# Attention followed by a SoLU layer: the transposed tiles come back from DRAM by one transfer into all 128 partitions

## The chip, the cores and the metric

The kernel runs on one core of a Trainium2 chip. The metric is the device time of one execution in microseconds (us), smaller is better. A profiled execution has its own time, and its span, from the first to the last instruction in the trace, lies a little below that.

## The reference, cut to what matters

```python
# chunked attention: 4 batches, 8 heads, 768 positions, 64 features per head
for c in range(nc):                      # chunks of 32 queries
    k_full = concat(mem_k, k[l_start:r_end])      # at most 8 + 16 + 32 + 8 = 64 keys
    scores = scale * q_c @ k_full.T
    a = exp(scores - max(scores)); a = a / (sum(a) + 1e-09)
    out[c] = a @ v_full
x = out as (3072 tokens, 512)
# SoLU layer with layer norm, d_ff = 1024
h = x @ w_in
solu = h * softmax(h)
ln = (solu - mean) / sqrt(var + 1e-06) * g_ln
return ln @ w_out                        # (3072, 512)
```

## The kernel before

The 3072 tokens are 24 tiles of 128. Attention is done by items: item 0 is tile 0, item 1 is tile 1, and each of the items 2 to 12 is two tiles. The two products of the SoLU layer are done tile by tile.

**Products in two parts.** The operands of `hidden` (x times w_in) and `project` (ln times w_out) are split into a rounded high part and a low part, both in the format fp32r, and each product is three matmuls: high by high, high by low, low by high. A tile has 8 such triples in `hidden` (four blocks of 128 features of x, two halves of 512 hidden columns) and 8 in `project`. In `hidden` the activations are the stationary operand and 512 columns of w_in the moving operand, which is read contiguously.

**Transposing.** Three kinds of data must have their features on the partitions before TensorE (PE) can use them: the probabilities p, the attention output x and the SoLU output u. Two ways exist.

- On PE, by a product with the identity (steps `PT`, `XT`, `UT`). The order uses it for the items 0 to 3 (p and x) and for u of the tiles 0 to 3.
- Through DRAM, for all else (9 items of p, 9 of x, 20 tiles of u, so 38 times). `square` lets VectorE (DVE) transpose every 32 x 32 block of the 128 x 1024 tile; `write` sends it to DRAM in one transfer of 512 KB; `read` brings it back in four transfers of 128 KB, the d-th into the partitions 32d to 32d+31. After that, partition 32d+n holds feature n of block d.

**Order.** The program text is a hand-written list of steps, `ORDER`, and every engine executes its own instructions in that order. Names in it: `Lq Lk Lv` loads of q, k, v; `S` scores, `M` row maximum, `Bm` subtracts it, `X` exponential, `Z` row sums; `Pt Pw Pr` (and `Xt Xw Xr`, `Ut Uw Ur`) square, write and read; `V` probabilities times values, `N` divides by the row sums; `XH XL UH UL` high and low parts; `G` one triple of `hidden`; `Hm He Hu` softmax of the hidden row; `C Sq Dn` centre, square and scale; `O` one triple of `project`; `Os St` scaling and store. The list names the engine of some steps by a letter: @V VectorE, @S ScalarE, @G GpSimd. The list is the same before and after.

**Queues.** Writes, reads and loads are all issued by SyncE (SP), one after the other in the order of the list. The stores of the output are issued by ScalarE. An issue waits on semaphores for its source and its buffer, and what is behind it on the same engine waits with it.

Lines that the change touches: 315 to 321 (`read`), 373 to 379 (`below_max`), 385 to 392 (`row_sum`), 424 to 431 (`norm`), 469 to 486 (`hidden`), and the host's layout of v, w_in and w_out.

Of the kernel before, what the change touches and what calls it, by code (L numbers as in the profile page):

```python
# [15 lines left out]
ALU = mybir.AluOpType  # L16
AX = mybir.AxisListType

P = 128
CHUNK, LEFT, RIGHT = 32, 16, 8  # L20
NEG = -1.0e30
SQ = 32
SLOTS, HALVES, RAWS, ROUNDED = 7, 6, 4, 8
SINGLES = 2
SPLIT = {0: 2}


# [2 lines left out]
ORDER = """  # L30
# [59 lines left out]
def chunked_attention_then_solu_kernel(  # L90
# [22 lines left out]
    nc = tc.nc  # L113
    D = P // 2
    NP_ = w_in.shape[0] // (2 * D)
    NT = out.shape[0] // P
    NCH = P // CHUNK
    LINE = kw.shape[0] // (NT * P * NP_)
    KEYS = P // 2
    DM, DF = w_in.shape  # L120
    items = [(t, 1) for t in range(SINGLES)] + [(t, 2) for t in range(SINGLES, NT, 2)]
    NC_ = DM // P
    NF = DF // P
    HALF = DF // 2
    TPB = 6
# [14 lines left out]
    away = {}  # L140
# [12 lines left out]
    def get(*key):  # L153
        return held[key][0]

    def used(*key):
        held[key][1] -= 1
        if held[key][1] == 0:
            buf, _, kind = held.pop(key)
            if kind == "raw":  # L160
                rest[0] -= 1
                if rest[0] < RAWS:
                    free["slot"].extend([buf[:, 0:W], buf[:, W:2 * W]])
                    return
            free[kind].append(buf)
# [13 lines left out]
    w_in_h = const.tile([P, NC_, DF], F32R, name="w_in_h")  # L179
    w_in_l = const.tile([P, NC_, DF], F32R, name="w_in_l")  # L180
# [66 lines left out]
    def cut(ap, i, x):  # L247
        n = ap.shape[1] // SPLIT.get(i, 1)
        return ap[:, x * n:(x + 1) * n]
# [4 lines left out]
    def w_load(i):  # L254
        raw = take("raw", ("raw", i), 2 * SPLIT.get(i, 1)).bitcast(U32)
        nc.sync.dma_start(raw, w_in32[i] if i < NC_ else w_out32[i - NC_])
# [39 lines left out]
    def home(i):  # L296
        return "slot" if items[i][1] == 2 else "half"
# [17 lines left out]
    def read(name):  # L315
        def step(i):
            t = get(name + "t", i).rearrange("p (q e) -> p q e", q=4)
            a = away[name, i].rearrange("(q n) (d e) -> q n d e", q=4, d=4)
            for d in range(4):
                nc.sync.dma_start(t[SQ * d:SQ * d + SQ], a[:, :, d].rearrange("q n e -> n q e"))  # L320
        return step

    def by_block(ap):
# [32 lines left out]
    def by_head(i):  # L356
        n = items[i][1]
        return get("s", i)[:, :, 0:n * HALF // 2].rearrange("p r (n k) -> p r n k", k=KEYS)

    def row_max(i):  # L360
# [9 lines left out]
        nc.vector.tensor_reduce(nmax, s, axis=AX.X, op=ALU.max, negate=True)  # L370
        used("s", i)

    def below_max(i):
        n = items[i][1]
        nmax = get("nmax", i)[:, 0:2 * n * NP_].rearrange("p (r n) -> p r n", r=2).unsqueeze(3)
        a = take(home(i), ("p", i), 2).rearrange("p (n r k) -> p r n k", r=2, k=KEYS)
        nc.vector.tensor_tensor(a, by_head(i), nmax.broadcast_to([P, 2, n * NP_, KEYS]), ALU.add)
        used("s", i)
        used("nmax", i)

# [3 lines left out]

    def row_sum(i):
        s = take("per_head", ("rinv", i), 1)[:, 0:2 * items[i][1] * NP_]
        nc.vector.tensor_reduce(  # L387
            s, get("p", i).rearrange("p (n k) -> p n k", k=KEYS), axis=AX.X, op=ALU.add
        )
        nc.vector.tensor_scalar(s, s, 1e-9, None, ALU.add)  # L390
        nc.vector.reciprocal(s, s)
        used("p", i)
# [31 lines left out]
    def norm(i):  # L424
        n = items[i][1]
        rinv = get("rinv", i)[:, 0:2 * n * NP_].rearrange("p (n r) -> p r n", r=2).unsqueeze(3)
        x = take(home(i), ("x", i), 1).rearrange("p (n r d) -> p r n d", r=2, d=D)
        xp = get("xp", i)[:, :, 0:n * HALF // 2].rearrange("p r (n k) -> p r n k", k=D)
        nc.vector.tensor_tensor(x, xp, rinv.broadcast_to([P, 2, n * NP_, D]), ALU.mult)
        used("xp", i)  # L430
        used("rinv", i)

# [36 lines left out]
    def hidden(t, c, half):  # L469
        if c == 0 and half == 0:  # L470
            take("two", ("h", t), 2)
        u, odd = divmod(t, 2)
        h = get("h", t)
        x = [
            get(n, u).rearrange("p (t c n) -> p t c n", t=2, n=P)[:, odd, c]
            for n in ("xh", "xl")
        ]
        w = (w_in_h, w_in_l)
        for i, (a, b) in enumerate(((0, 0), (0, 1), (1, 0))):
            nc.tensor.matmul(  # L480
                h[:, half], x[a], w[b][:, c, half * HALF:(half + 1) * HALF],
                start=c == 0 and i == 0, stop=c == NC_ - 1 and i == 2,
            )
        if c == NC_ - 1 and half == 1:
            used("xh", u)
            used("xl", u)
# [65 lines left out]
    def store(t):  # L552
# [24 lines left out]
def _layout(q, k, v, mem_k, mem_v):  # L577
    import numpy as np

    B, H, S, D = q.shape  # L580
    M = mem_k.shape[2]
    NPAIR = H // 2
    NCH = S // CHUNK
    KEYS = M + LEFT + CHUNK + RIGHT
    TPB = S // P
    CPT = P // CHUNK
    NT = B * TPB

    qT = q.reshape(B, NPAIR, 2, TPB, P, D).transpose(0, 3, 2, 5, 1, 4)
    qT = qT.reshape(NT, 2 * D, NPAIR, P)  # L590

    def padded(x):
        z = np.zeros((B, H, LEFT, D), x.dtype)
        return np.concatenate([z, x, z[:, :, :RIGHT]], 2)

    kp, vp = padded(k), padded(v)

    lines = []
    for t in range(TPB):
        x = kp[:, :, t * P:t * P + P + LEFT + RIGHT]  # L600
        mid = P - CHUNK
        lines.append(np.concatenate([x[:, :, :CHUNK], mem_k, x[:, :, CHUNK:mid], mem_k, x[:, :, mid:]], 2))
    kw = np.stack(lines, 1).reshape(B, TPB, NPAIR, 2, -1, D).transpose(0, 1, 3, 5, 2, 4)
    kw = kw.reshape(NT, 2 * D, NPAIR, -1)

    wins = []
    for c in range(NCH):
        x = vp[:, :, c * CHUNK:c * CHUNK + KEYS - M]
        e = 0 if c % 2 else CHUNK
        wins.append(np.concatenate([x[:, :, :e], mem_v, x[:, :, e:]], 2))  # L610
    vw = np.stack(wins, 2).reshape(B, NPAIR, 2, TPB, CPT, KEYS, D).transpose(0, 3, 2, 5, 1, 4, 6)
    vw = vw.reshape(NT, 2 * KEYS, NPAIR, CPT, D)
    def by_item(x):
        n = x.shape[0]
        late = x[SINGLES:].reshape((n - SINGLES) // 2, 2, P, -1).transpose(0, 2, 1, 3)
        return np.concatenate([x[:SINGLES].ravel(), late.ravel()])

    return by_item(qT), by_item(kw), by_item(vw)
# [28 lines left out]
```

## Time and profile before

| what | value |
|---|---|
| median of 3 runs | 359.84 us (356.36 to 359.94) |
| profiled execution, its own time | 359.48 us |
| span of its trace | 357.7 us |
| PE busy in it | 325.8 us |
| DVE busy in it | 219.7 us |

PE is TensorE's matmuls, PEld its loads of the stationary operand, DVE is VectorE, ACT ScalarE, POOL GpSimd, SP SyncE; SPq is SyncE issuing transfers. L312 is line 312 of the kernel. Names of buffers stand without their numbers, as out<-in. [...]

### The profile page before, as it was taken

The page shows a single profiled execution, that of the slowest core. Times are in us where ns is not written, and L with a number is a line of the kernel's source. Part 1 is how long each engine was busy: PE and PEld are TensorE (multiplying, and loading weights), DVE is VectorE, ACT ScalarE, POOL GpSimd, SP SyncE. Part 2 cuts the span into 40 slices and gives each one's busy share as a digit, 9 for nine tenths or more (in the row PEclk, how much of TensorE's full clock was granted, in tenths as well). Part 3 has the DMA queues.
Part 4 walks back from the last instruction along what each step waited for, and adds up shares of the span by engine and source line. Part 5 has one row for each costly group of instructions (what it writes and reads, how often), then busy time and mean ns, then how long its engine had stood idle before and what let it go on. Part 6 is the DMA issues. An engine that isn't in the chain of part 4 may idle for free.

```text
span 357.7 us, 9973 instructions
## 1 busy us (share of the span) xinstructions
PE 325.8 (91%) x4324; PEld 263.7 (74%) x4324; DVE 219.7 (61%) x264; ACT 130.0 (36%) x189; POOL 138.9 (39%) x173
## 2 busy tenths in 40 slices
PE   1569999999997999979999899999959999999995
PEld 1557887888785877857887678888647888888884
DVE  1589999968966964756955386564466654037300
ACT  3256375542422414122322334422225064232521
POOL 0226061442318263752500834220523746625160
PEclk9969999999998999998999999999969999999999
DMA  7999925576897876689959679866651547435621
GB/s 296 420 422 400 405 78 199 198 252 192 302 306 218 245 267 214 220 233 353 268 191 263 194 216 382 286 188 188 212 210 60 184 114 226 128 129 173 226 90 59
DMA packets 37771, 82.31 MB, mean 230 GB/s; under 512 B 4320, under 2 KB 23776, under 8 KB 35296
## 3 DMA queue, kind: packets, MB, share of 16 engines
q1 hardware_dynamic: 34272, 75.39, 62.8%
q10 hardware_dynamic: 3456, 6.29, 4.7%
q8 instruction: 34, 0.56, 0.6%
q14 instruction: 9, 0.07, 0.1%
HBM read 55.45 MB, written 26.21 MB: 228 GB/s over the span
## 4 chain that ended last, share of the span: by engine, by line
PE 61%; DMA 18%; DVE 12%; SPq 3%; ACT 3%; issue 2%; POOL 1%; DVEq 0%; POOLq 0%; ACTq 0%
PE one L540 28%; PE two L480 23%; DMA out<-half 5%; PE two L347 4%; PE two L415 3%; SPq L320 3%; DMA q<-in_qT 2%; DMA raw<-p_away 2%; DMA k<-in_kw 2%; DVE per_head L387 2%; DMA p_away<-raw 2%; DMA raw<-x_away 1%; DMA slot<-x_away 1%; PE two L203 1%; PE two L333 1%
## 5 line engine op out<-in xcount | busy, mean ns | idle before, releaser
L480 PE MATMUL two<-w_in_h,fr 128*128 128x512 f32 x384 | 143.0, 405 | 6.8 <-DVE fr L219 4.6
L540 PE MATMUL one<-w_out_h,fr 128*128 128x512 f32 x384 | 138.1, 396 | 0.1
L480 PEld LDWEIGHTS two<-w_in_h,fr 128*128 128x128 f32 x384 | 73.4, 192 | 26.1 <-DVE fr L219 5.4
L540 PEld LDWEIGHTS one<-w_out_h,fr 128*128 128x128 f32 x384 | 72.7, 189 | 16.8 <-DVE fr L219 0.5
L480 PE MATMUL two<-w_in_l,fr 128*128 128x512 f32 x192 | 76.2, 397 | 0.2 <-DVE w_in_l L219 0.2
L540 PE MATMUL one<-w_out_l,fr 128*128 128x512 f32 x192 | 75.2, 391 | 0.0
L489 DVE TENSOR_REDUCE per_row<-two 128x1 f32<-128x1024 f32 x24 | 29.1, 1212 | 28.9 <-PE two L480 28.8
L548 ACT ACTIVATE half<-one,per_row 128x512 f32<-128x512 f32 x24 | 16.5, 687 | 82.2 <-PE one L540 80.8
L480 PEld LDWEIGHTS two<-w_in_l,fr 128*128 128x128 f32 x192 | 36.9, 192 | 7.7 <-DVE w_in_l L219 0.6
L540 PEld LDWEIGHTS one<-w_out_l,fr 128*128 128x128 f32 x192 | 36.5, 190 | 7.3
L219 POOL TENSOR_TENSOR fr<-raw,fr 128x1024 fp32r<-128x1024 f32 x13 | 31.2, 2403 | 17.4 <-ACT fr L214 16.6
L347 PE MATMUL two<-k,q 64*32 64x64 f32 x1536 | 19.6, 237 | 14.5 <-DMA k<-in_kw 7.6
L347 PEld LDWEIGHTS two<-k,q 64*32 64x32 f32 x1536 | 17.1, 111 | 18.8 <-issue 17.9
L216 POOL TENSOR_SCALAR fr<-raw 128x1024 fp32r<-128x1024 f32 x11 | 11.6, 1051 | 47.1 <-DVE slot L304 18.1
L219 POOL TENSOR_TENSOR fr<-slot,fr 128x1024 fp32r<-128x1024 f32 x9 | 21.5, 2391 | 18.1 <-DMA slot<-u_away 10.7
L494 ACT ACTIVATE slot<-two,per_row 128x1024 f32<-128x1024 f32 x12 | 13.4, 1118 | 30.6 <-DVE per_row L489 30.6
L494 ACT ACTIVATE raw<-two,per_row 128x1024 f32<-128x1024 f32 x12 | 13.4, 1115 | 27.7 <-DVE per_row L489 21.4
L216 POOL TENSOR_SCALAR fr<-slot 128x1024 fp32r<-128x1024 f32 x8 | 8.4, 1052 | 32.4 <-DMA slot<-u_away 15.3
L504 DVE CUSTOM_DVE_ANT_0 slot<-two,slot 128x1024 f32<-128x1024 f32 x12 | 14.7, 1222 | 8.1 <-ACT slot L494 8.1
L504 DVE CUSTOM_DVE_ANT_0 raw<-two,raw 128x1024 f32<-128x1024 f32 x12 | 14.5, 1206 | 7.7 <-ACT raw L494 6.2
L370 DVE TENSOR_REDUCE per_head<-two 128x16 f32<-128x1024 f32 (+1 forms) x13 | 14.8, 1135 | 5.0 <-PE two L347 4.7
L304 DVE STREAM_TRANSPOSE raw<-slot 128x1024 f32<-128x1024 f32 x10 | 12.4, 1238 | 8.1 <-POOL slot L516 5.9
(88 smaller groups left out, 372.9 us busy)
## 6 DMA issues: line engine op xcount, KB each, us to landing
v<-in_vw SPq DMA_DIRECT2D x11, 1024.0 KB, 8.5
k<-in_kw SPq DMA_DIRECT2D x11, 672.0 KB, 6.8
out<-half ACTq DMA_DIRECT2D x24, 256.0 KB, 3.0
u_away<-raw SPq DMA_DIRECT2D x12, 512.0 KB, 3.5
raw<-u_away SPq DMA_DIRECT2D x48, 128.0 KB, 3.4
q<-in_qT SPq DMA_DIRECT2D x11, 512.0 KB, 7.8
raw<-in_w_in SPq DMA_DIRECT2D x4, 1024.0 KB, 11.3
raw<-in_w_out SPq DMA_DIRECT2D x4, 1024.0 KB, 9.2
```

What stands on the lines that cost most here:

```text
L216: nc.gpsimd.tensor_scalar(out, in_, 1.0, 0.0, ALU.mult, ALU.add)
L219: (nc.gpsimd if on == "G" else nc.vector).tensor_tensor(out, a, b, ALU.subtract)
L304: nc.vector.transpose(t, src.rearrange("p (m d n) -> p d m n", d=4, n=SQ))
L320: nc.sync.dma_start(t[SQ * d:SQ * d + SQ], a[:, :, d].rearrange("q n e -> n q e"))
L347: nc.tensor.matmul(s[32 * j:32 * j + 32, r, t, g], q[rows, o + t, g, 32 * j:32 * j + 32], k[rows, o + t, g, START[j]:START[j] + KEYS], sta ...
L370: nc.vector.tensor_reduce(nmax, s, axis=AX.X, op=ALU.max, negate=True)
L480: nc.tensor.matmul(h[:, half], x[a], w[b][:, c, half * HALF:(half + 1) * HALF], start=c == 0 and i == 0, stop=c == NC_ - 1 and i == 2,)
L489: nc.vector.tensor_reduce(take("per_row", ("hm", t), 1), flat(get("h", t)), axis=AX.X, op=ALU.max, negate=True)
L494: nc.scalar.activation(take("slot", ("u", t), 2), flat(get("h", t)), AF.Exp, bias=get("hm", t), scale=1.0, accum_out=take("per_row", ("esu ...
L504: nc.vector.tensor_tensor_reduce(u, flat(get("h", t)), u, 1.0, 0.0, ALU.mult, ALU.add, accum_out=usum)
L540: nc.tensor.matmul(get("o", t), u[a], w[b][:, f], start=f == 0 and i == 0, stop=f == NF - 1 and i == 2)
L548: nc.scalar.mul(take("half", ("osb", t), 1), get("o", t), get("rstd", t))
```

## The change

`read` issues one transfer instead of four. With 128 rows in DRAM seen as (q n) and 1024 columns as (d e), the transfer takes (n d) as its partitions, so that feature n of block d comes to partition 4n+d. The pieces in it are 1 KB long, as they were. The features are thus in another order on the partitions than those of tiles transposed on PE, and the rest of the change makes up for that:

- The host permutes the rows of w_in and, per block of 128, its columns, so that x and u read back from DRAM find the right weights; w_out and g_ln stay in their order.
- For items that go through DRAM, `below_max` writes the probabilities in an order of runs of 16 that puts the two heads of a pair back on 64 partitions each; it becomes two instructions of half the size, and so does the reduction in `row_sum`. The host permutes v to match for all tiles but the first six.
- For x of the items 0 to 3, transposed on PE, `norm` becomes two instructions of half the size, which write with a step of four words (16 bytes).
- For the tiles 0 to 3, whose u is transposed on PE, `hidden` reads the same 512 columns of w_in in another order: successive elements lie 32 words (128 bytes) apart, four of them, and then the next group begins one word on.

```diff
@@ read
-            a = away[name, i].rearrange("(q n) (d e) -> q n d e", q=4, d=4)
-            for d in range(4):
-                nc.sync.dma_start(t[SQ * d:SQ * d + SQ], a[:, :, d].rearrange("q n e -> n q e"))
+            nc.sync.dma_start(t, away[name, i].rearrange("(q n) (d e) -> (n d) q e", q=4, d=4))
@@ below_max
-        a = take(home(i), ("p", i), 2).rearrange("p (n r k) -> p r n k", r=2, k=KEYS)
-        nc.vector.tensor_tensor(a, by_head(i), nmax.broadcast_to([P, 2, n * NP_, KEYS]), ALU.add)
+        a = take(home(i), ("p", i), 2)
+        if f"PT{i}" in todo:
...
+        else:
+            a = a.rearrange("p (n d r m) -> p r n d m", d=4, r=2, m=KEYS // 4)
+            for r in range(2):
+                nc.vector.tensor_tensor(
+                    a[:, r], by_head(i)[:, r].rearrange("p n (d m) -> p n d m", d=4),
+                    nmax[:, r].unsqueeze(3).broadcast_to([P, n * NP_, 4, KEYS // 4]), ALU.add,
+                )
@@ row_sum
+            a = get("p", i).rearrange("p (n d r m) -> p r n d m", d=4, r=2, m=KEYS // 4)
+            for r in range(2):
+                nc.vector.tensor_reduce(
+                    s.rearrange("p (n r) -> p r n", r=2)[:, r], a[:, r], axis=AX.XY, op=ALU.add
+                )
@@ norm
+        if f"XT{i}" in todo:
+            x = x.rearrange("p (n m r a) -> p r n a m", m=SQ, r=2, a=2)
+            for r in range(2):
+                nc.vector.tensor_tensor(
+                    x[:, r], xp[:, r].rearrange("p n (a m) -> p n a m", a=2),
+                    rinv[:, r].unsqueeze(3).broadcast_to([P, n * NP_, 2, SQ]), ALU.mult,
+                )
@@ hidden
-        w = (w_in_h, w_in_l)
+        w = [m[:, c, half * HALF:(half + 1) * HALF] for m in (w_in_h, w_in_l)]
+        if f"UT{t}" in todo:
+            w = [m.rearrange("p (f d n) -> p f n d", d=4, n=SQ) for m in w]
@@ host
+    place = np.arange(KEYS)
+    place = KEYS // 4 * (place % 4) + place // 4
+    vw = vw.reshape(NT, 2, KEYS, NPAIR, CPT, D)
+    vw = np.concatenate([vw[:AHEAD], vw[AHEAD:, :, place]])
...
+    block = np.arange(P)
+    there, here = 4 * (block % SQ) + block // SQ, SQ * (block % 4) + block // 4
+    hidden = np.arange(DF).reshape(-1, P, 2).transpose(0, 2, 1)
+    column = hidden[:, :, there].ravel()
+    row = np.arange(H * D).reshape(-1, P)[:, here].ravel()
```

## Rows read from the trace of the kernel before

**Rows 1.** The page's busy time: us, share of the span, instructions.
```profile
PE 325.8 (91%) x4324; PEld 263.7 (74%) x4324; DVE 219.7 (61%) x264; ACT 130.0 (36%) x189; POOL 138.9 (39%) x173
```

**Rows 2.** Busy time by stretch: PE, PEld, DVE, ACT, POOL; then clock, DMA.
```profile
28.20:60.30 32.10, 31.23 (x516) 24.88 (x513) 30.74 (x38) 18.96 (x25) 10.78 (x9) 1.00 0.72 277
150.00:170.00 20.00, 16.71 (x318) 13.51 (x307) 13.01 (x15) 4.90 (x7) 8.68 (x9) 0.91 0.90 289
262.90:265.60 2.70, 2.69 (x6) 2.16 (x7) 1.43 (x2) 1.58 (x3) 0.00 (x0) 0.50 0.47 134
270.00:350.00 80.00, 80.00 (x475) 65.91 (x474) 31.26 (x38) 31.14 (x47) 40.26 (x58) 1.00 0.44 149
```

**Rows 3.** PE's waits from 100 us on: us in total, times, longest.
```profile
PE two L480 <- DVE fr L219: 4.1, 1, 4.1
PE two L347 <- DMA q<-in_qT: 3.3, 1, 3.3
PE two L415 <- DMA raw<-p_away: 2.3, 2, 1.4
PE two L480 <- POOL fr L219: 1.4, 1, 1.4
```

**Rows 4.** SyncE's issues in order of time: start us, us, what, how many.
```profile
105.05 2.63 SPq L320 DMA_DIRECT2D raw<-p_away  x4
...
151.96 2.12 SPq L320 DMA_DIRECT2D slot<-p_away  x4
...
154.60 0.43 SPq L232 DMA_DIRECT2D q<-in_qT  x1
...
241.70 6.91 SPq L320 DMA_DIRECT2D slot<-u_away  x4
248.97 0.34 SPq L312 DMA_DIRECT2D x_away<-slot  x1
...
262.94 1.74 SPq L320 DMA_DIRECT2D raw<-p_away  x4
```

**Rows 5.** SyncE's own waits from 60 to 345 us.
```profile
SPq L320 <- DMA out<-half: 31.5, 8, 6.5
```

**Rows 6.** Matmuls in order of time: start us, us, what.
```profile
28.19 0.48 PE L480 MATMUL two<-w_in_h,fr 128*128 128x512 f32 x1
...
36.12 0.39 PE L480 MATMUL two<-w_in_l,fr 128*128 128x512 f32 x1
36.35 0.40 PE L480 MATMUL two<-w_in_h,fr 128*128 128x512 f32 x1
...
60.07 0.39 PE L480 MATMUL two<-w_in_h,fr 128*128 128x512 f32 x1
...
263.93 0.63 PE L480 MATMUL two<-w_in_l,fr 128*128 128x512 f32 x1
264.35 1.05 PE L480 MATMUL two<-w_in_h,fr 128*128 128x512 f32 x2
```

**Rows 7.** Instructions by form: busy us, mean ns, then idle before.
```profile
L521 ACT ACTIVATE slot<-slot 128x1024 f32<-128x1024 f32 x12 | 12.6, 1048 | 5.6 <-DVE raw L304 5.6
...
L429 DVE TENSOR_TENSOR slot<-two,per_head 128x1024 f32<-128x1024 f32 x7 | 8.5, 1214 | 13.2 <-PE two L415 9.5 <-DMA raw<-x_away 3.7
...
L273 DVE SCALAR_TENSOR_TENSOR slot<-raw,slot 128x1024 uint32<-128x1024 uint32 x5 | 7.1, 1415 | 0.1
...
L260 ACT ACTIVATE slot<-raw 128x1024 f32<-128x1024 f32 x5 | 5.6, 1141 | 2.7 <-DMA raw<-in_w_in 2.7
...
L429 DVE TENSOR_TENSOR half<-two,per_head 128x512 f32<-128x512 f32 x2 | 1.4, 692 | 0.8 <-PE two L415 0.8
```

**Rows 8.** The page's DMA issues: count, KB each, median us to landing.
```profile
u_away<-raw SPq DMA_DIRECT2D x12, 512.0 KB, 3.5
raw<-u_away SPq DMA_DIRECT2D x48, 128.0 KB, 3.4
...
x_away<-raw SPq DMA_DIRECT2D x4, 512.0 KB, 6.4
```

More of the change, by code (lines that the diff above doesn't have):

```diff
@@ L24 @@
 SINGLES = 2
+AHEAD = 6
 SPLIT = {0: 2}
@@ L371, in row_max @@
         used("s", i)
+    todo = set(ORDER.split())
     def below_max(i):
@@ L375, in below_max @@
         nmax = get("nmax", i)[:, 0:2 * n * NP_].rearrange("p (r n) -> p r n", r=2).unsqueeze(3)
-        a = take(home(i), ("p", i), 2).rearrange("p (n r k) -> p r n k", r=2, k=KEYS)
-        nc.vector.tensor_tensor(a, by_head(i), nmax.broadcast_to([P, 2, n * NP_, KEYS]), ALU.add)
+        a = take(home(i), ("p", i), 2)
+        if f"PT{i}" in todo:
+            a = a.rearrange("p (n r k) -> p r n k", r=2, k=KEYS)
+            nc.vector.tensor_tensor(a, by_head(i), nmax.broadcast_to([P, 2, n * NP_, KEYS]), ALU.add)
+        else:
[5 more added lines that the diff above has]
+                )
         used("s", i)
@@ L386, in row_sum @@
         s = take("per_head", ("rinv", i), 1)[:, 0:2 * items[i][1] * NP_]
-        nc.vector.tensor_reduce(
-            s, get("p", i).rearrange("p (n k) -> p n k", k=KEYS), axis=AX.X, op=ALU.add
-        )
+        if f"PT{i}" in todo:
+            nc.vector.tensor_reduce(s, get("p", i).rearrange("p (n k) -> p n k", k=KEYS), axis=AX.X, op=ALU.add)
+        else:
+            a = get("p", i).rearrange("p (n d r m) -> p r n d m", d=4, r=2, m=KEYS // 4)
[3 more added lines that the diff above has]
+                )
         nc.vector.tensor_scalar(s, s, 1e-9, None, ALU.add)
@@ L426, in norm @@
         rinv = get("rinv", i)[:, 0:2 * n * NP_].rearrange("p (n r) -> p r n", r=2).unsqueeze(3)
-        x = take(home(i), ("x", i), 1).rearrange("p (n r d) -> p r n d", r=2, d=D)
         xp = get("xp", i)[:, :, 0:n * HALF // 2].rearrange("p r (n k) -> p r n k", k=D)
-        nc.vector.tensor_tensor(x, xp, rinv.broadcast_to([P, 2, n * NP_, D]), ALU.mult)
+        x = take(home(i), ("x", i), 1)
+        if f"XT{i}" in todo:
[5 more added lines that the diff above has]
+                )
+        else:
+            x = x.rearrange("p (n r d) -> p r n d", r=2, d=D)
+            nc.vector.tensor_tensor(x, xp, rinv.broadcast_to([P, 2, n * NP_, D]), ALU.mult)
         used("xp", i)
@@ L477, in hidden @@
         ]
-        w = (w_in_h, w_in_l)
+        w = [m[:, c, half * HALF:(half + 1) * HALF] for m in (w_in_h, w_in_l)]
+        if f"UT{t}" in todo:
+            w = [m.rearrange("p (f d n) -> p f n d", d=4, n=SQ) for m in w]
         for i, (a, b) in enumerate(((0, 0), (0, 1), (1, 0))):
             nc.tensor.matmul(
-                h[:, half], x[a], w[b][:, c, half * HALF:(half + 1) * HALF],
+                h[:, half], x[a], w[b],
                 start=c == 0 and i == 0, stop=c == NC_ - 1 and i == 2,
@@ L610, in _layout @@
         wins.append(np.concatenate([x[:, :, :e], mem_v, x[:, :, e:]], 2))
-    vw = np.stack(wins, 2).reshape(B, NPAIR, 2, TPB, CPT, KEYS, D).transpose(0, 3, 2, 5, 1, 4, 6)
+    wins = np.stack(wins, 2)
+    vw = wins.reshape(B, NPAIR, 2, TPB, CPT, KEYS, D).transpose(0, 3, 2, 5, 1, 4, 6)
+    place = np.arange(KEYS)
+    place = KEYS // 4 * (place % 4) + place // 4
+    vw = vw.reshape(NT, 2, KEYS, NPAIR, CPT, D)
+    vw = np.concatenate([vw[:AHEAD], vw[AHEAD:, :, place]])
     vw = vw.reshape(NT, 2 * KEYS, NPAIR, CPT, D)
@@ L628 @@
     DF = moe_g_ln.shape[0]
-    column = np.arange(DF).reshape(-1, P, 2).transpose(0, 2, 1).ravel()
-    g = moe_g_ln[column].reshape(-1, P).T
-    w_in, w_out = (np.ascontiguousarray(w).view(np.uint64) for w in (moe_w_in[:, column], moe_w_out))
+    block = np.arange(P)
[3 more added lines that the diff above has]
+    row = np.arange(H * D).reshape(-1, P)[:, here].ravel()
+    g = moe_g_ln[hidden.ravel()].reshape(-1, P).T
+    w_in, w_out = (np.ascontiguousarray(w).view(np.uint64) for w in (moe_w_in[row][:, column], moe_w_out))
     ins = dict(zip(_INS, (qT, kw, vw, w_in, w_out, g)))
```

## The prediction

> **What bounds the kernel now.** I read the page's busy shares first: PE has something in flight for 91% of the span and nobody else comes near it [rows 1]. A share over the whole span hides stages, so I asked for stretches next. From 270 to 350 us PE is busy for 80.00 of 80 us at full clock, and the kernel ends by PE working off its queue [rows 2]. The stretch from 28.2 to 60.3 us is different: PE is busy for 31.23 of 32.1 us, and DVE for 30.74 of the same 32.1 [rows 2]. There two engines are full at once, and work added to either has nowhere to hide. Third, PE's own waits. After 100 us only four places are worth a name, together 11.1 us: 4.1 us for a low part made by DVE, 3.3 us for a load of q, 2.3 us in two waits for probabilities read back, 1.4 us for a low part made by GpSimd [rows 3]. That is nearly the whole stock out of which faster reads can pay. What comes on top is the clock behind such a wait: in the 2.7 us after the longest one the granted clock was 0.50, the lower level [rows 2].
>
> **The change part by part.**
>
> *The reads.* Each of the 38 reads becomes one issue in place of four. Four issues that nothing stops take 1.74 us, one about 0.43 [rows 4], so SyncE has 1.3 us less to do per read, 38 x 1.3 = 50 us in all. Nearly all of it is beside PE's work; it counts only where PE waits. Landing: the fourth of the small transfers lands at about 1.3 + 3.4 = 4.7 us after the first issue [rows 4, 8]. The trace shows no read of 512 KB in pieces of 1 KB. Its nearest rows are the writes of 512 KB, 3.5 us at best and 6.4 us at worst [rows 8], so a read comes between 1.2 us sooner and 1.7 us later. I take 1.2 to 1.3 us sooner: the bytes and pieces are the same, and the small transfers of 128 KB took 3.4 us, about as long as the quick write of four times the size.
>
> Second effect: within a group of four, issues are stopped by transfers that have nothing to do with them. The group at 241.70 took 6.91 us instead of 1.74, and the write of x behind it left only at 248.97 [rows 4]. In total the reads' line waited 31.5 us, in eight places, for stores of the output [rows 5]. I read this as reuse of a semaphore, since the reads need nothing of the output; four times fewer issues put four times more of the program between one use and the next.
>
> What the four places give. The q load at 154.60 stands behind a group of 2.12 us [rows 4]: 1.7 of its 3.3 us go, and about half of the slow clock around it. (The clock of 0.91 over those 20 us is 3.6 us at the lower level, a loss of 1.8 us [rows 2].) So 2.6 us. Two waits for probabilities lose up to 1.3 us each: 2 us. The 4.1 us wait comes at the end of a path that starts with the write held up until 248.97; I take 3.5 us, with part of the slow clock behind it. The 1.4 us wait: 1.3 us. Sum 9.4, say 9.5 us. Bounds: 14 us if all four waits and 3 us of slow clock go; a loss of 7 us if each read lands 1.7 us later in four places. After these waits PE is next itself, so nothing more can come out.
>
> *`hidden` of the tiles 0 to 3.* 4 tiles x 24 = 96 matmuls read w_in with successive words 128 bytes apart. All of them lie between 28.19 and 60.3 us [rows 6], in the stretch where PE is full, so each added nanosecond is on the path. The trace has no stepped operand on PE, so the price has to be bounded. Below: nothing. A gain is excluded, since the same 512 columns pass. Contiguous matmuls start 0.23 us apart (36.12 and 36.35 [rows 6]). Other engines do show that steps cost: ScalarE reading every second word took 1141 ns against 1048 for a contiguous tile of that size, VectorE 1415 against 1214 [rows 7], 9% and 17% at a step of only 8 bytes. Above: a full column per word fetched at the pace of VectorE, 692 ns for 512 columns [rows 7], 0.46 us more per matmul, 44 us. Between them: PE takes a word every 0.45 ns, while ScalarE and VectorE with contiguous words take about one per 1.0 and 1.2 ns [rows 6, 7]. PE's pace thus looks like more than one word per fetch. If a stepped read gives it one word per fetch at half its pace, the matmul costs what it costs at the lower clock, 0.42 us (263.93 to 264.35, clock 0.50 [rows 2, 6]). I take that: 96 x (0.42 - 0.23) = 18.2 us. It is the nearest row in kind, the same instruction at half its rate.
>
> [...]
>
> *VectorE.* Halving an instruction costs 2 x 692 - 1214 = 170 ns [rows 7]. `norm` of the items 0 to 3 pays it four times, 0.7 us, in or next to the full stretch, and its writes with a step of 16 bytes may cost as L273 does (17% of some 3.8 us, 0.6 us). I put 1 us on the path. `below_max` and `row_sum` of nine items pay 18 x 0.17 = 3.1 us after 60 us, where PE sets the end; cover is PE's queue, and if it were gone a third of a microsecond per item would stand in the way of the exponential. Loads, host permutations and the number of matmuls cost nothing: same bytes, same counts.
>
> *Sum*, against the profiled execution, 359.48 us (0.1% under the median of 359.84): 359.5 + 18.2 + 1 - 9.5 = 369.2, **369 us**, 2.7% slower.
>
> **The rivals.**
>
> *Steps are free on PE (351 us, chance 0.33).* PE fetches stepped words at its full rate, and the reads' gain is what remains: 359.5 + 1 - 9.5 = 351. [...] Against it: the 9% and 17% of the other engines. It decides from the point where 96 matmuls cost less than the 8.5 us that the rest gives, 0.09 us each: spacing under 0.32 us makes the change faster, above it slower.
>
> *Each stepped word costs a fetch at another engine's pace (395 us, chance 0.27).* 44 us in place of 18: 359.5 + 44.4 + 1 - 9.5 = 395, and more if a fetch is slower still. For it: VectorE's rate for single words is the only one that I can read, and its steps of two words already slow it. Against it: PE shows 2.2 words per ns, so its path is wider. [...]
>
> *The one transfer lands no sooner.* Then the 9.5 us shrink to the issue time alone or vanish, and with half rate the time is 372 to 378. This lies within the forecast's case: the half rate as a whole has a chance of 0.40 and reaches from 358 to 380.
>
> **How the numbers follow.** About 1% (3.6 us) is what a measurement here can tell from no change. Case one, 0.40: same 0.07, slower 0.33. Steps free, 0.33: faster 0.30, same 0.03. Slow fetch, 0.27: all slower. Together faster 0.30, same 0.10, slower 0.60. The range starts where the gain reaches most of its bound with free steps, 347, and goes through the slow fetch to 405, leaving some 0.05 below and 0.13 above. Since the cases have both signs: the forecast's own range is 358 to 380.
>
> **What would show it.** Start to start of the matmuls at L480 up to about 60 us, 0.42 us against 0.23 after, at an unchanged clock: the half rate. 0.23: free steps. 0.7: slow fetch. The first matmul of `project` at L540 comes some 18 us later than 60.30 with the forecast. In SyncE's rows one issue of about 0.43 us stands for each group of four; waits of the reads' line for stores of the output should fall far below 31.5 us. PE's four waits should lose some 6 us. I'm wrong if the matmuls keep their spacing, if DVE becomes the one that PE waits for between 28 and 60 us, or if the single reads take 6 us to land and PE's waits grow.

## The result, and the profile after

The changed kernel takes 345.63 us (median of 4 runs, 345.42 to 346.83) where the kernel before takes 359.81 us (4 runs, 356.36 to 359.94): a ratio of 0.9635, 95% interval 0.9573 to 0.9696. It is faster by 3.65%. Some executions of a kernel run in a slower state than the rest, and the ratios here and below leave these out, so a ratio need not be the quotient of the two medians beside it. The prediction was 369 us, slower, with a range from 347 to 405; both the sign and the range are wrong. The profiled execution took 345.63 us, and its span is 343.8 us, 13.9 us less than the span before.

The page's busy times and its chain, by engine. PE's busy time is 3.2 us less than before and its idle time (span less busy) fell from 31.9 to 21.2 us [rows 1]; the chain that ended last (its shares are the second line, and those of the kernel before the third) is now PE nearly throughout.

```profile
PE 322.6 (94%) x4324; PEld 261.0 (76%) x4324; DVE 222.6 (65%) x286; ACT 130.3 (38%) x189; POOL 139.0 (40%) x173
...
PE 94%; issue 2%; DMA 2%; DVE 1%; ACT 0%; SPq 0%
...
PE 61%; DMA 18%; DVE 12%; SPq 3%; ACT 3%; issue 2%; POOL 1%; DVEq 0%; POOLq 0%; ACTq 0%
```

The stretches of [rows 2] up to 270 us, and those between them; columns as there (PE, PEld, DVE, ACT, POOL; then the mean of TensorE's granted clock, which is 1.00 or 0.50 at every moment of both traces; DMA share, GB/s).

```profile
28.20:60.30 32.10, 32.10 (x501) 23.09 (x500) 30.17 (x38) 16.16 (x21) 10.24 (x8) 1.00 0.65 252
60.30:110.30 50.00, 47.05 (x937) 37.94 (x936) 40.58 (x54) 19.76 (x28) 16.05 (x20) 0.97 0.71 247
110.30:150.00 39.70, 39.70 (x581) 32.42 (x582) 30.38 (x39) 14.64 (x23) 25.35 (x32) 1.00 0.73 258
150.00:170.00 20.00, 20.00 (x427) 16.34 (x420) 15.83 (x22) 4.94 (x7) 8.66 (x9) 1.00 0.97 330
170.00:270.00 100.00, 99.89 (x1166) 81.83 (x1164) 67.18 (x83) 35.77 (x52) 40.96 (x49) 1.00 0.67 234
```

From 110 to 270 us PE is idle for 0.1 us and the granted clock is 1.00. The same three stretches before, of which [rows 2] shows the middle one:

```profile
110.30:150.00 39.70, 36.78 (x636) 29.33 (x635) 26.25 (x33) 12.30 (x20) 22.12 (x31) 0.96 0.71 229
...
170.00:270.00 100.00, 93.49 (x1025) 74.76 (x1013) 60.20 (x70) 29.62 (x45) 31.63 (x35) 0.97 0.73 232
```

That is 2.9 + 3.3 + 6.5 = 12.7 us of idle PE and a granted clock of 0.96, 0.91 and 0.97, a loss of 1.6 + 1.8 + 3.0 = 6.4 us, an estimate from the mean clock of each stretch. All of it is gone. Of PE's waits from 28 to 100 us one is left, which the trace gives no releaser for (the profile's "issue"), and after 100 us there is none; [rows 3] has no row to stand against. This one wait, at 93.4 us, with the clock behind it, is new: it costs 2.95 us of idle time and 1.5 us of clock (0.97) in the stretch from 60.3 to 110.3 us. It stands in the middle of the matmuls of one `V` step, 67 instructions before it and 61 after it, and waits for "issue" at this step are in five of the forms with single reads that follow here, 2.2 us in e3_contig, 2.5 in e4_small, 2.8 in e5_center, 2.9 in e9_after_pool and 3.3 in e12_after_mixed; what PE waits for there stays open.

```profile
PE two L430 <- issue: 3.0, 1, 3.0
```

SyncE's issues in order of time, at about the place of the group of 6.91 us in [rows 4]: one issue per read, and none is stopped.

```profile
235.47 0.33 SPq L313 DMA_DIRECT2D x_away<-slot  x1
238.25 0.36 SPq L319 DMA_DIRECT2D slot<-x_away  x1
238.66 0.59 SPq L319 DMA_DIRECT2D raw<-u_away  x1
```

SyncE's own waits. The reads (L319) wait for the writes of the same tile and for nothing of the output; the only row with out<-half is the end of the program. Before, the reads' line waited 31.5 us for the output's stores [rows 5].

```profile
SPq L319 <- DMA u_away<-raw: 21.6, 8, 6.5
SPq L678 <- DMA out<-half: 20.1, 1, 20.1
```

The matmuls of `hidden` in the tiles 0 to 3 (L506), start us, us, and the first of `project` (L566). From 40.72 to 41.53 are 0.81 us for three, 0.27 us each, at a granted clock of 1.00, against 0.23 in [rows 6]. `project` starts at 62.63 us, 2.3 us after the 60.30 of the kernel before.

```profile
40.72 0.44 PE L506 MATMUL two<-w_in_l,fr 128*128 128x512 f32 x1
40.99 0.71 PE L506 MATMUL two<-w_in_h,fr 128*128 128x512 f32 x2
41.53 0.44 PE L506 MATMUL two<-w_in_l,fr 128*128 128x512 f32 x1
...
62.63 0.40 PE L566 MATMUL one<-w_out_h,fr 128*128 128x512 f32 x1
```

DVE's instructions by form: `norm` with steps of 16 bytes (L447), and the two halves of `below_max` (L384) and `row_sum` (L402).

```profile
L384 DVE TENSOR_TENSOR raw<-two,per_head 128x512 f32<-128x512 f32 x12 | 7.7, 685 | 0.2
L402 DVE TENSOR_REDUCE per_head<-raw 128x8 f32<-128x512 f32 x12 | 7.5, 668 | 0.0
...
L447 DVE TENSOR_TENSOR half<-two,per_head 128x256 f32<-128x256 f32 x4 | 2.2, 637 | 0.6 <-PE two L430 0.5
...
L447 DVE TENSOR_TENSOR raw<-two,per_head 128x512 f32<-128x512 f32 x2 | 2.0, 1090 | 0.0
L447 DVE TENSOR_TENSOR slot<-two,per_head 128x512 f32<-128x512 f32 x2 | 2.0, 1078 | 0.0
```

The page's issues of the reads, median us to landing. The medians of the single read of 512 KB are 4.6 to 6.0 us, no less than the four together took (1.3 us until the fourth was issued, and 3.4 [rows 4, 8]).

```profile
raw<-u_away SPq DMA_DIRECT2D x12, 512.0 KB, 4.6
...
slot<-p_away SPq DMA_DIRECT2D x4, 512.0 KB, 6.0
raw<-x_away SPq DMA_DIRECT2D x4, 512.0 KB, 5.8
```

### The profile page after: what moved, and what is told of

Its sections match the earlier page's. It is cut to its first block, busy times and chain, and to the rows that moved or that the text cites. A ratio compares the mean times of both kernels' runs of the same rounds, so it can differ in the third digit from the quotient of the medians.

```text
span 343.8 us, 9779 instructions
## 1 busy us (share of the span) xinstructions
PE 322.6 (94%) x4324; PEld 261.0 (76%) x4324; DVE 222.6 (65%) x286; ACT 130.3 (38%) x189; POOL 139.0 (40%) x173
## 4 chain that ended last, share of the span: by engine, by line
PE 94%; issue 2%; DMA 2%; DVE 1%; ACT 0%; SPq 0%
PE two L506 40%; PE one L566 39%; PE two L430 5%; PE two L346 5%; PE two L332 2%; DMA k<-in_kw 2%; PE two L204 1%; PE one L332 1%; DVE half L447 0%; DVE half L380 0%; DVE per_head L369 0%; ACT half L574 0%; ACT half L393 0%; SPq L233 0%; SPq L257 0%
## 5 line engine op out<-in xcount | busy, mean ns | idle before, releaser
L506 PE MATMUL two<-w_in_h,fr 128*128 128x512 f32 x384 | 141.5, 402 | 0.0
L566 PE MATMUL one<-w_out_h,fr 128*128 128x512 f32 x384 | 137.9, 395 | 0.0
L506 PEld LDWEIGHTS two<-w_in_h,fr 128*128 128x128 f32 x384 | 72.1, 188 | 18.3 <-DVE fr L220 0.3
L566 PEld LDWEIGHTS one<-w_out_h,fr 128*128 128x128 f32 x384 | 72.6, 189 | 16.5 <-ACT half L574 0.3
L506 PE MATMUL two<-w_in_l,fr 128*128 128x512 f32 x192 | 76.5, 398 | 0.0
L566 PE MATMUL one<-w_out_l,fr 128*128 128x512 f32 x192 | 75.4, 392 | 0.0
L506 PEld LDWEIGHTS two<-w_in_l,fr 128*128 128x128 f32 x192 | 36.1, 188 | 8.3 <-DVE w_in_l L220 0.4
L566 PEld LDWEIGHTS one<-w_out_l,fr 128*128 128x128 f32 x192 | 36.4, 189 | 7.2
L220 POOL TENSOR_TENSOR fr<-raw,fr 128x1024 fp32r<-128x1024 f32 x13 | 31.5, 2425 | 9.3 <-ACT fr L215 8.5
L346 PE MATMUL two<-k,q 64*32 64x64 f32 x1536 | 18.6, 229 | 10.9 <-DMA k<-in_kw 7.4
L346 PEld LDWEIGHTS two<-k,q 64*32 64x32 f32 x1536 | 16.3, 107 | 15.1 <-issue 14.3
L217 POOL TENSOR_SCALAR fr<-slot 128x1024 fp32r<-128x1024 f32 x8 | 8.4, 1047 | 25.9 <-issue 14.3
L555 POOL TENSOR_SCALAR per_row<-per_row,per_row 128x1 f32<-128x1 f32 x24 | 6.4, 265 | 30.1 <-ACT raw L547 19.5
```

What stands on the lines that cost most here:

```text
L217: nc.gpsimd.tensor_scalar(out, in_, 1.0, 0.0, ALU.mult, ALU.add)
L220: (nc.gpsimd if on == "G" else nc.vector).tensor_tensor(out, a, b, ALU.subtract)
L346: nc.tensor.matmul(s[32 * j:32 * j + 32, r, t, g], q[rows, o + t, g, 32 * j:32 * j + 32], k[rows, o + t, g, START[j]:START[j] + KEYS], sta ...
L506: nc.tensor.matmul(h[:, half], x[a], w[b], start=c == 0 and i == 0, stop=c == NC_ - 1 and i == 2,)
L566: nc.tensor.matmul(get("o", t), u[a], w[b][:, f], start=f == 0 and i == 0, stop=f == NF - 1 and i == 2)
```

## The experiments

So the gain does not come from earlier landings. Three accounts of it were open. **Semaphores:** reads no longer stand behind stores of the output. **Issues:** SyncE has 114 issues fewer to make, whatever they wait for. **Shape:** transfers into 128 partitions go better than those into 32.

The first can be read in the compiled programs and in the traces, where each transfer names the semaphore that it raises (a counter that tells when the transfer has landed). SyncE's transfers and ScalarE's stores share eight of them in strict turn, in the order in which the program places them (each has 32 or 33 of the 262 transfers of the kernel before). No transfer was issued before the one that used its semaphore eight places earlier, one turn, had landed: in the trace of the kernel before, 254 have such a one, in that of the changed kernel 140, and the closest follows its landing by 0.01 us. Where that was a store, a read stands behind a store, although it needs nothing of it. In the trace of the kernel before, eight reads are issued 0.01 to 0.02 us after the landing of the store that had their semaphore (one at 248.31 us, its store landing at 248.29); these are the eight waits of [rows 5]. The other nine of its 17 are issued 2.3 to 10.1 us after it. GpSimd's 24 stores in e8_before_pool take eight other semaphores. Counted:

```
kernel                                   in turn   reads one turn behind a store
before                                     262            17
after                                      148             5
after, four transfers of 32 partitions     262            17
after, four transfers by columns           262            12
after, three small loads per read          262             3
any form with all stores by GpSimd     238 or 124           0
```

**Issues or shape: four transfers in place of one.** Two forms of the changed kernel with the old number of issues:

```diff
-            nc.sync.dma_start(t, away[name, i].rearrange("(q n) (d e) -> (n d) q e", q=4, d=4))
+            a = away[name, i].rearrange("(q n) (d e) -> (n d) q e", q=4, d=4)
+            for d in range(4):                                             # e1_four
+                nc.sync.dma_start(t[32 * d:32 * d + 32], a[32 * d:32 * d + 32])
...
+            for k in range(4):                                             # e2_fourq
+                nc.sync.dma_start(t[:, k], a[:, k])
```

Expected of the four by partitions:

> The changed kernel with each read cut again into four transfers of 32 partitions, in the new order of partitions; everything else stays changed. Theory A (the number of issues: SyncE's time and its waits for the semaphores of unrelated transfers made PE wait): the waits come back, 359.5 plus 4.4 us for the stepped matmuls, so 358 to 365 us, and SyncE's reads wait again for stores of the output for 20 to 30 us. Theory B (the layout of the transfer: a single read into all 128 partitions lands sooner): also 358 to 365 us, since each piece again fills 32 partitions only; but then without long waits for the stores. Theory C (the gain comes from another part of the change): 344 to 347 us.

Measured: 357.83 us (10 runs, 352.2 to 363.19), 0.9914 of the kernel before (0.986 to 0.9968). The waits for stores are back, and with them PE's waits for reads of probabilities, 2.9 us. SyncE's wait row of this kernel:

```profile
SPq L321 <- DMA out<-half: 30.3, 8, 8.5
```

Expected of the four by columns:

> The changed kernel with each read cut into four transfers of 128 KB, each into all 128 partitions and one quarter of their columns. Theory A (number of issues): 358 to 365 us, as with four transfers of 32 partitions. Theory B (all 128 partitions at once): 344 to 348 us. If it lies between, both have a part.

Measured: 345.29 us (340.91 to 347.96), ratio 0.9615 (0.9519 to 0.9711), as fast as the single read. Its rows of SyncE: the wait for stores, and groups of four that take 1.74 us and more, as before.

```profile
SPq L321 <- DMA out<-half: 0.4, 1, 0.4
```
```profile
232.44 1.74 SPq L321 DMA_DIRECT2D raw<-u_away  x4
234.23 2.53 SPq L321 DMA_DIRECT2D slot<-u_away  x4
```

The two differ in the partitions that a transfer fills, and also in the places that the compiler gives the stores among SyncE's transfers. The number of issues is the same, so the account by issues falls. Twelve reads still stand one turn behind a store in e2_fourq and yet wait 0.4 us in all: what counts is whether that store has landed by then, not the count. Shape and semaphores are not told apart by this pair.

**Semaphores alone.** In the kernel before, and in the changed one, the stores are issued by GpSimd and nothing else is changed.

```diff
-        nc.scalar.dma_start(out[t * P:(t + 1) * P, :], get("osb", t))
+        nc.gpsimd.dma_start(out[t * P:(t + 1) * P, :], get("osb", t))
```

> The kernel before, four transfers per read, with one change: the stores of the output are issued by GpSimd instead of ScalarE. In the built program the transfers of SyncE and ScalarE take the same eight semaphores in turn, and 17 reads stand one turn behind a store; GpSimd's transfers have semaphores of their own, so no read stands behind a store any more. Theory A1 (the reads wait for stores through shared semaphores, and this is most of what the change removed): 342 to 348 us, with four issues per read as before and no stepped matmuls. Theory A2 (SyncE's time for the issues is what counts): 355 us or more. GpSimd's issues may cost some us of their own, since its queue waits for each scaled output.

Measured: 345.74 us (344.68 to 351.94) beside 356.72 us for the kernel before, ratio 0.973 (0.9662 to 0.9798), with four issues per read, transfers into 32 partitions and no stepped operand. No read waits for a store. PE's waits from 100 us on in this kernel, against [rows 3], and its stretches from 110 to 270 us:

```profile
PE two L347 <- DMA q<-in_qT: 1.1, 1, 1.1
PE two L415 <- DMA raw<-p_away: 0.9, 1, 0.9
PE one L540 <- POOL fr L219: 0.6, 2, 0.4
```
```profile
110.30:150.00 39.70, 38.80 (x654) 31.51 (x653) 31.25 (x39) 13.62 (x22) 24.68 (x33) 1.00 0.79 250
150.00:170.00 20.00, 18.29 (x322) 14.77 (x322) 15.75 (x20) 6.45 (x9) 8.61 (x9) 1.00 1.04 323
170.00:270.00 100.00, 99.61 (x1165) 81.42 (x1164) 62.72 (x74) 34.15 (x51) 45.62 (x57) 1.00 0.75 238
```

The two waits of `hidden` for low parts, 4.1 and 1.4 us [rows 3], are gone (0.6 us are left at `project`, L540), and q's is 1.1 instead of 3.3. PE is idle for 3.0 us from 110 to 270 us instead of 12.7, and the clock is 1.00 throughout. This is the experiment that decides: shape and number of the reads stay, and most of the gain is there. One rival it leaves without a run of its own: the edit also takes the stores off ScalarE. That is unlikely to be the gain, since the 24 issues took 0.34 to 0.48 us each in the kernel before, with ScalarE busy for 36% of the span [rows 1], and none of PE's waits in [rows 3] ended on ScalarE.

> The changed kernel with the stores issued by GpSimd. Theory A1: no read waits for a store in the changed kernel already, so nothing is left to win: 344 to 348 us; a value above 348 is what GpSimd's issues cost, and belongs off the result of the same edit in the kernel before.

Measured: 348.77 us (347.28 to 350.24), ratio 0.9825 (0.9752 to 0.9899), about 3 us slower than the changed kernel in its own runs. Its reads did not wait for stores anyhow, and GpSimd's issuing has a price: one issue takes 0.60 us there (mean of 24 in e8_before_pool, 14.3 us in all), against 0.34 to 0.48 us on ScalarE in the kernel before. At the end of the chain of the changed kernel with GpSimd's stores there are rows that the other does not have:

```profile
335.23 4.86 issue
340.11 0.63 POOL out L579
340.74 0.65 issue
```

**Is the tail all of that price?** The first 18 stores by GpSimd, the last six, which no read follows, by ScalarE:

```diff
+        at_end = t in (13, 19, 20, 21, 22, 23)
-        nc.scalar.dma_start(out[t * P:(t + 1) * P, :], get("osb", t))
+        (nc.scalar if at_end else nc.gpsimd).dma_start(out[t * P:(t + 1) * P, :], get("osb", t))
```

> The kernel before, with the stores of the first 18 tiles in the list issued by GpSimd and those of the last six (19, 13, 20 to 23), which no read follows, by ScalarE as before. Theory A (the gain comes from reads that no longer wait for a store's semaphore; the tail with GpSimd's stores gives some 3 us back): no read waits for out<-half, no stepped matmul, and the end as in the kernel before, so some 341 to 344 us, faster than the changed kernel. Rival (four issues per read cost SyncE what they did, and the gain is not free of them): 346 to 350, no better than the changed kernel.

Measured: 348.53 us (6 runs, 346.1 to 351.19), ratio 0.975 (0.9689 to 0.9811). A miss: no better than with all stores by GpSimd, and 3 us behind the changed kernel in the same set (e11_after_again, below). PE waits 2.1 us for q and 0.7 us for probabilities in it, and a group of four issues that takes 2.73 us still stands in front of the loads of k and q; why the tail gave nothing back stays open.

> The changed kernel with its stores divided as in the mixed form of the kernel before: 18 by GpSimd, the last six by ScalarE. Theory A: only five reads stand behind a store in the changed kernel and none of them waited in its profile, so there is nothing to gain; GpSimd's 18 issues cost little outside of the tail: 344 to 347 us. Rival (reads behind stores do cost the changed kernel something in most executions): 340 to 343 us.

Measured: 348.34 us (345.19 to 349.37), ratio 0.973 (0.9677 to 0.9782): a miss too, some 3 us slower than the changed kernel. The price of GpSimd's stores is thus not only in the tail. It is about what e8_before_pool (345.74 us) lacks against the single read without the step (342.68 us, e3_contig below), so shape and number of issues need have no part of their own in the gain; this is an estimate across sets, and no run shows it by itself.

> The changed kernel once more, beside the others of this set on the same chip: 345 to 347 us, 0.96 to 0.97 of the kernel before.

Measured: 345.46 us (345.07 to 349.54), ratio 0.9687 (0.9627 to 0.9746), as expected. No form tried with all parts of the computation in place was shown to beat the changed kernel; e2_fourq and e8_before_pool come level with it.

**More transfers in the turn, without more reads.** Behind each single read, three loads of 512 bytes that nothing needs:

```diff
             nc.sync.dma_start(t, away[name, i].rearrange("(q n) (d e) -> (n d) q e", q=4, d=4))
+            for _ in range(3):
+                nc.sync.dma_start(spare[:, count[0]:count[0] + 1], g_ln[:, 0:1])
+                count[0] += 1
```

> The changed kernel with three loads of 512 bytes behind each single read, which nothing waits for: the number of issues and of semaphores taken is that of before, while the reads stay single. Theory A (number of issues): 354 to 365 us, SyncE's waits for stores of the output come back. Theory B (landing of the read itself): 344 to 348 us.

Measured: four runs between 347.53 and 356.92 us (median 354.33), too far apart for a ratio. In the profiled one (353.63 us) waits for stores are back, most of them at the small loads (L324):

```profile
SPq L324 <- DMA out<-half: 8.3, 4, 4.4
...
SPq L322 <- DMA out<-half: 1.9, 1, 1.9
```

The direction fits the semaphores, but the small loads also bring work of their own; this one settles nothing.

**What the stepped operand costs.** The kernel before with the reading order of the change in the tiles 0 to 3, whose hidden columns then come out in another order:

```diff
-        w = (w_in_h, w_in_l)
+        w = [m[:, c, half * HALF:(half + 1) * HALF] for m in (w_in_h, w_in_l)]
+        if t < 4:
+            w = [m.rearrange("p (f d n) -> p f n d", d=4, n=SQ) for m in w]
```

> The kernel before with only the stepped reading of w_in in the tiles 0 to 3, so that their hidden columns are in another order than w_out's rows. 96 matmuls at 0.045 us more are 4.4 us. If PE is the bound in that stretch and the later waits stay: 362 to 364 us. If waits later in the kernel take it up: 358 to 360 us.

Measured: 359.71 us (358.34 to 364.06), ratio 1.0121 (1.0042 to 1.02): 1.5 to 7.1 us slower, around the 4.3 us that 96 matmuls of 0.27 instead of 0.227 us add. The waits for stores stay, at 30.2 us, and `project` starts at 63.06 us, 2.8 us later than in the kernel before. And the changed kernel without the step, again with hidden columns in another order:

```diff
-        if f"UT{t}" in todo:
-            w = [m.rearrange("p (f d n) -> p f n d", d=4, n=SQ) for m in w]
```

> The changed kernel with w_in read contiguously for the tiles 0 to 3 too, so that their hidden columns come out in another order than w_out's rows have. If the stepped matmuls cost 0.272 - 0.227 = 0.045 us each and PE is the bound from 28 us on, 96 of them are 4.4 us: 341 to 342 us. If other waits of the early stretch take their place (DVE is as full there): 344 to 346 us.

Measured: 342.68 us (340.64 to 343.26), ratio 0.9608 (0.9551 to 0.9664): some 3 us below the changed kernel, less than the 4.3. `project` starts at 59.80 us, 2.8 us before that of the changed kernel. In the full stretch VectorE is now busy for 31.57 of 32.10 us, PE for 31.77, and the chain runs over VectorE from 26.65 to 55.37 us. That VectorE holds back the rest of the 4.3 us is likely by this, but not shown: PE's named waits there come to no more than 0.5 us.

```profile
28.20:60.30 32.10, 31.77 (x518) 25.25 (x516) 31.57 (x41) 19.11 (x25) 11.85 (x9) 1.00 0.72 281
```

The contiguous reading again, with the permutation moved to where u is centred, so that no column is out of its place (two tiles on ScalarE, two on GpSimd, the input read in steps of 32 words, the output written in order):

```diff
+        if f"UT{t}" in todo:
...
+            u = u.rearrange("p (f d n) -> p f n d", d=4, n=SQ)
+            out = out.rearrange("p (f n d) -> p f n d", d=4, n=SQ)
-            nc.scalar.activation(u, u, AF.Identity, bias=nmu, scale=1.0)
+            nc.scalar.activation(out, u, AF.Identity, bias=nmu, scale=1.0)
```

> The changed kernel with contiguous reading of w_in everywhere; for the tiles 0 to 3 the centring step writes u in the other order into another buffer instead (two on ScalarE, two on GpSimd), reading with a step of 32 words. If PE's 4.4 us are all on the path and the four centring steps are beside it: 341 to 343 us. If a stepped centring step takes twice its 1.1 us and stands in the chain that PE waits for: 343 to 346 us.

Measured: 347.35 us (6 runs, 345.85 to 348.08), ratio 0.9775 (0.9727 to 0.9824), no better than the changed kernel. The step costs these engines about twice their time: ScalarE 2227 ns against 1149, GpSimd 2112 against 1128. The rows by form, of each engine the contiguous one first:

```profile
L547 POOL TENSOR_SCALAR raw<-raw,per_row 128x1024 f32<-128x1024 f32 x4 | 4.5, 1128 | 7.1 <-DVE per_row L531 7.1
...
L545 ACT ACTIVATE raw<-raw,per_row 128x1024 f32<-128x1024 f32 x3 | 3.4, 1149 | 5.9 <-DVE per_row L531 5.9
...
L545 ACT ACTIVATE raw<-slot,per_row 128x1024 f32<-128x1024 f32 x1 | 2.2, 2227 | 0.0
...
L547 POOL TENSOR_SCALAR slot<-raw,per_row 128x1024 f32<-128x1024 f32 x1 | 2.1, 2112 | 0.0
```

**What in the step costs.** One run of a kernel in which ten more tiles read w_in in an order of their own, `w[b].rearrange("p (a s) -> p s a", s=...)` for the steps, `"p (a s two) -> p s a two"` for the last two:

> The changed kernel, in which the tiles 8 to 17 also read their 512 columns of w_in in another order, each with a step of its own between successive elements: 2, 4, 8, 16, 32, 64, 128 and 256 words for the tiles 8 to 15; tile 16 reads pairs of words that lie 32 words apart, tile 17 runs of four words that lie 32 words apart. The hidden columns of these tiles come out in another order, so only the times of the matmuls count. Theory S (a matmul pays for every element that doesn't lie in the same 16 bytes as the one before): 0.227 us for one matmul at no step, a little more at 2 words, about 0.27 us from 4 words on whatever the step, the pairs half of the surplus, the runs of four none. Theory D (the price is that of the step of 128 bytes, or of a larger one alone): 0.227 us up to 16 words, 0.27 us at 32, and more at 64 to 256. Theory N (the surplus is that of a read order with a second dimension, whatever the step): 0.27 us for all ten tiles.

Three matmuls in a row, from its chain in order of time (start us, us, line), at a granted clock of 1.00: L513 reads with a step of 2 words, L516 4, L519 8, L525 32, L528 64, L531 128, L534 256, L537 pairs and L540 runs of four that lie 32 words apart; L600 is contiguous.

```profile
129.48 1.35 PE two L513 x3
130.84 1.39 PE one L600 x6
132.22 1.38 PE two L516 x3
...
152.03 1.29 PE two L519 x3
...
195.49 1.55 PE two L528 x3
197.04 1.30 PE two L525 x3
...
229.38 0.65 PE two L534 x3
...
230.72 0.82 PE two L531 x3
...
242.05 0.73 PE two L540 x3
...
252.54 1.39 PE two L537 x3
```

A matmul takes 0.23 us contiguous; 0.45, 0.46, 0.43, 0.43, 0.43 and 0.52 us at steps of 2, 4, 8, 16 (L522, 1.30 for three), 32 and 64 words; 0.27 at 128, 0.22 at 256; pairs 0.46, runs of four 0.24. None of the three theories has this. Not the step decides, as far as the orders of single words go, but how many words one pass of the inner loop touches before the next pass comes back beside the first: 512 divided by the step, so 256 words down to 8 for the doubled prices, 4 at a step of 128 (0.27) and 2 at a step of 256 (0.22). The order in the change has 4 words in its inner pass, 32 words apart, and costs 0.27 like the step of 128, whereas the same step of 32 words with 16 in a pass costs 0.43; this is the one step at which two lengths of a pass were measured. The runs of four do not fit this: with 64 words in a pass they are nearly at the contiguous price (0.24), while the pairs, with 32 in a pass, cost 0.46. Why a return after four words is cheap and after eight is not, no run shows. Summed over 24 matmuls for each tile, the surplus is some 40 us, and the span is 41.6 us longer.

**Does anything else of the change help?** e1_four, with the step, came out at 357.83 us, no slower than the kernel before in its set (358.38); if the step cost it 4.3 us, other parts of the change would have to give some 5 us. So e1_four without the step, beside e3_contig once more:

```diff
-        if f"UT{t}" in todo:
-            w = [m.rearrange("p (f d n) -> p f n d", d=4, n=SQ) for m in w]
...
+            for d in range(4):
+                nc.sync.dma_start(t[32 * d:32 * d + 32], a[32 * d:32 * d + 32])
```

> The changed kernel with each read as four transfers of 32 partitions and with w_in read contiguously in the tiles 0 to 3 as well (their hidden columns come out in another order): the feature order, the two-instruction steps and the weights of the changed kernel, but neither its single read nor its stepped matmuls. 17 reads stand one turn behind a store, as in the kernel before. Theory A (waits for the stores' semaphores, and nothing else of the change, made the difference): the time of the kernel before, 356 to 360 us, with reads that wait for out<-half some 30 us. Theory B (something else of the change gives some 5 us, since the form with four transfers and stepped matmuls came to 357.83 us where the kernel before with the same stepped matmuls came to 359.71): 350 to 354 us with the same waits.

Measured: 358.37 us (6 runs, 357.6 to 361.16) beside 357.3 us for the kernel before, ratio 1.014 (1.0046 to 1.0235). No gain of another part of the change shows; the waits for stores are those of before:

```profile
SPq L321 <- DMA out<-half: 29.6, 7, 7.7
```

> The changed kernel with w_in read contiguously in the tiles 0 to 3, a second time, beside the form with four transfers: 341 to 344 us by both theories. Its distance to the form with four transfers is what the single read gives when no matmul is stepped: 14 to 17 us by theory A, 8 to 11 us by theory B.

Measured: 343.43 us (342.12 to 344.77), ratio 0.9704 (0.9632 to 0.9776), 14.9 us below the form with four transfers: what the single read gives when no matmul is stepped, as the account by semaphores expects. That e1_four, with the step, lies no higher than e14_four_contig, without it, stays unexplained; kernels with these waits scatter widely (the kernel before from 351.16 to 360.92 us in this set, e1_four from 352.2 to 363.19), the changed one from 345.07 to 349.54.

## Why the prediction was wrong

**Where PE is full (28 to 60 us): the place was right.** The stepped matmuls all lie before the first `project`, and what they add shows: `project` starts 2.3 us later, and 2.8 us later in e7_before_step, which has the step alone.

**The price of the stepped matmuls: the term was mis-sized.** 18.2 us were put for 96 matmuls at half rate, 0.42 us each. They take 0.27, so the term is 4.3 us by spacing, and 2 to 3 us by the time (345.46 against 343.43 us, 345.63 against 342.68, each pair from two sets), probably because VectorE is as full as PE in the same stretch (31.57 of 32.10 us in e3_contig). The prediction named 0.32 us as the spacing that decides the sign; 0.27 is on the fast side. Its half rate is not wrong as such: with 8 stepped words or more in the inner pass a matmul does cost 0.43 to 0.52 us. The error was to take "128 bytes apart" for the whole description, when the text of the change says that after four words the next group begins one word on.

**The reads: right in kind, mis-sized, and from another cause.** 9.5 us were forecast, with 14 as the bound. With the other terms as measured (359.5 + 4.3 from the spacing, to 345.6) the reads must have given some 18 us; the pair without the step gives 14.9 (358.37 against 343.43 us). Three things in that step failed. First, landing: it was taken as 1.2 to 1.3 us sooner, and it is no sooner (4.6 to 6.0 us for one, 4.7 for four). Second, issue time: it counted 1.3 us per read where PE waits, but e2_fourq has four issues per read and is as fast as the changed kernel. Third, the stock out of which reads can pay: it was put at four named waits, 11.1 us, and little of the clock, with 14 us as the bound. All four waits went, and the stretches from 110 to 270 us held 12.7 us of idle PE and 6.4 us of slow clock, 19.1 in all; [rows 2] shows only the middle one of the three.

**Reuse of a semaphore: seen, and priced at one wait only.** The prediction read the 31.5 us of waits [rows 5] rightly as reuse of a semaphore by unrelated stores, but let it enter only through the write held up until 248.97. The run e8_before_pool shows that it carries most of the gain: with the stores' semaphores apart and nothing else changed, the ratio is 0.973 (0.9662 to 0.9798), and the two waits of `hidden` for low parts, 5.5 us before [rows 3], are gone. Such a wait holds up more than its read: the group at 241.70 took 6.91 us where its issues need 1.74 [rows 4], and what is behind it on SyncE goes late, the write of x at 248.97.

**VectorE.** The term was 1 us, from 1.3 us of work. `norm` of the items 0 to 3 went from 2 x 0.69 + 2 x 1.21 = 3.8 us [rows 7] to 4 x 0.64 + 4 x 1.08 = 6.9 us: 3.1 us, since the writes in steps of 16 bytes cost 1.08 us per 512 columns where 17% on 0.69 were assumed. As PE is the fuller one in the same stretch (28.2 to 60.3: DVE busy 30.17, PE 32.10), it does not show by itself.

**Where the 13.9 us are.** From 110 to 270 us: 19.1 us gained less 0.1. From 60 to 110 us: 2.8 us of idle time and 1.5 us of clock lost at the wait at 93.4 us, whose releaser the trace does not give. The stepped matmuls: 4.3 us lost, less the 0.9 us of idle PE from 28 to 60 us that is gone. Together 11.3 us; the remaining 2.6 us are not assigned to a place.

**The rivals.** The time came out nearest to the rival with free steps (351 us, chance 0.33), though the steps are not free. What it lacked is the size of the reads' gain; that it came nearest is luck in part, since its condition, steps at no cost, did not hold.

## What to carry to other kernels

A queue's wait for something that it does not need, here 31.5 us for the stores, is a cost to price at once: count the semaphores in turn, and find out what stands one turn ahead of each load. It was taken away here by fewer transfers (345.63 us) and by another issuing engine (345.74 us, e8_before_pool). The change from 262 to 148 transfers in the turn also moved the pairings, from 17 reads behind a store to 5, so read the waits again afterwards. A stepped operand has to be priced by its whole reading order, not by its step: with the same step of 32 words a matmul took 0.27 us with 4 words in a pass and 0.43 with 16.

## What the runs showed of the hardware

A matmul with 512 columns of fp32r as the moving operand took, at a granted clock of 1.00 (e6_steps, and the changed kernel for 4 words 128 bytes apart), 0.227 to 0.232 us contiguous and 0.43 to 0.52 us with steps of 2 to 64 words (8 or more words per inner pass), but 0.27 with 4 words in the inner pass (128 or 512 bytes apart) and 0.217 with 2 words 1 KB apart, a little less than contiguous. ScalarE and GpSimd took about double (e5_center: 2227 against 1149 ns, 2112 against 1128) for the very order that cost TensorE a fifth (0.27 against 0.227 us). One read of 512 KB into 128 partitions landed no sooner (medians of 4.6 to 6.0 us) than four of 128 KB into 32 partitions issued one after the other (1.3 + 3.4 us). SyncE's and ScalarE's transfers share eight semaphores in turn in these programs (32 or 33 transfers on each in the kernel before), and a read waited up to 6.5 us for a store it has nothing to do with [rows 5].
